# Windowed attention feeding a feed-forward block: wider input rows, block means on TensorE, a fused exponential, 120-column score products and a new instruction order

## The chip, the cores and the metric

The kernel runs on one core of one Trainium2 chip. A core has five engines with a queue each: TensorE (PE in the profile; its weight loads are PEld), VectorE (DVE), ScalarE (ACT), GpSimd (POOL) and SyncE (SP), which here issues every DMA. Each queue runs in order and waits for the others by semaphores. The metric is device time in microseconds (us), as a median of runs. All times in this part come from the kernel before the change: 655.01 us, median of 3 runs (654.32 to 655.39).

## What is computed

The reference has two parts, one behind the other. In numpy, cut to what matters:

```python
# q, k, v: (4, 8, 768, 64) fp32: batch, heads, tokens, head size
k_sum = k.reshape(B, H, 24, 32, 64).max(axis=3)      # 24 blocks of 32 tokens
v_sum = v.reshape(B, H, 24, 32, 64).mean(axis=3)
scores_l = scale * q @ k.T         # kept where |i - j| < 16, else -1e9
scores_s = scale * q @ k_sum.T + np.log(32)
a = softmax(concat([scores_l, scores_s]))            # the sum + 1e-9 divides
attn = a @ concat([v, v_sum])
x = attn.transpose(0, 2, 1, 3).reshape(3072, 512)
h = x @ w_in                       # (512, 2048)
out = (h * np.cos(h)) @ w_out      # (2048, 512)
```

So every query looks at its near tokens and at 24 summaries of the whole sequence; the result is the input of a feed-forward layer with a cosine gate.

## The kernel before

**Tiles.** The 3,072 tokens are cut into 8 blocks of 384; blocks 0 and 1 are the two halves of batch 0. The 8 heads are taken two at a time, so a block has four *groups*, which the order table calls `a`, `b`, `c`, `d`: `c0` is the third pair of heads in block 0. A group's 384 queries are cut into 6 tiles of 64. Each tile sees a window of 96 keys (64 and 16 on either side) and the 24 summaries, 120 columns in all.

**A group's steps**, with the names of the order table and the lines of the kernel before: load q, k, v (`q`, `k`, `v`, L436 to L479); turn q and k so that the head size lies on partitions (`tq`, `tk`, PE transposes with an identity, L493 and L506; from group `b2` on DVE does it in 32x32 squares); copy them out of PSUM (`cq`, `ck`), q times the scale; take the maxima of the k blocks (`ks`, L527); for blocks 0 and 1 put the mask into PSUM by a product with the identity (`ms`, L547); the scores (`sc`, L560); copy or scale them to SBUF (`z`); their maximum (`mx`, L579); subtract it on POOL (`su`, L584); the exponential on ACT (`ex`, L597); the row sums on DVE (`sm`, L600); their inverse (`iv`, L605); multiply by it on POOL (`nm`, L608); turn the probabilities (`tp` on PE and `cp`, or `pt`, `po`, `pi` by way of DRAM); the product with v (`va`, L661); and the split of the result into a high and a low part in a reduced fp32 format (`xh`, `xl`). The scores are two products for a tile and head, one with 96 keys and one with 24 summaries:

```python
for lo, n, key in ((0, W, k0), (W, NB, KW)):        # W = 96, NB = 24
    nc.tensor.matmul(out=self.sp[hh][s*QT:(s+1)*QT, c, lo:lo+n],
                     lhsT=self.qd[rows, t*QT:(t+1)*QT], rhs=self.kd[rows, key:key+n], ...)
```

The four combinations of head (64 partitions in) and tile parity (64 partitions out) use the four 64x64 quarters of TensorE. A value product uses all partitions in and 64 out, so two of them fit side by side.

**Summaries of v.** For batch 0, `v0_0` and `v0_1` load v once more with one block of 32 tokens in a partition (L248), POOL adds the two halves (L253) and DVE sums the rest (L263). Each group then fetches its 24 rows, repeated for 6 tiles, with two DMAs (`m`, L484). For batches 1 to 3 the loads come in quarters and POOL sums most of them.

**Weights.** w_in and w_out arrive as 64-bit floats. For each of 16 slices `w0` to `w15`, six steps on ACT, DVE and POOL (`ab`, `cl`, `sh`, `lb`, `fb` and then `hi`, `lo`) make two reduced fp32 parts out of 1 MB of raw bits.

**Feed-forward.** 128 steps `s0` to `s127`, one for a slice of 128 hidden columns and a block of tokens. `up` is 12 products with 384 columns (L705); then ACT, DVE, ACT, DVE form the gate (`tu` L715, `re` L718, `si` L723, `ga` L727), the result is split into `hi` and `lo`, and `dh`, `dl` are 9 products with 512 columns (L756). `s0` to `s5` and `s22` to `s31` are block 0, `s6` to `s21` block 1. The first `up` in the order is `s1`, and it needs all four groups of block 0 and the weight slice `w1`.

**Order.** The program records instructions by hand, in the order of one long table of tokens (`ORDER`); an engine runs its instructions in the order in which the table names them. `a0.tk.1.3` means: group a0, turn k, second half, PSUM bank 3; a last letter a, v or p says ACT, DVE or POOL.

Of the kernel before, what the change touches and what calls it, by code (L numbers as in the profile page):

```python
# [10 lines left out]
F32 = mybir.dt.float32  # L11
# [7 lines left out]
FUSED = "00000000000000000000000000000000"  # L19
# [14 lines left out]
w1.cl.v c0.iv a0.tp.1.0 d0.tq.1 w1.sh.2.3 d0.cq.a d0.ms.4.5 d0.sc a0.tp.0.1 w1.lb w1.fb.1 w0.ab.0 c0.nm c0.tp.0.2
w0.cl.v w1.hi.v w1.lo.p w0.sh.6.7 w0.lb a0.cp.1.a a0.cp.0.a d0.z.0.a b1.q a0.m w2.sh.0.1 w2.ab.0 d0.z.1.v d0.mx d0.su
a0.va.3 c0.tp.1.4 w0.fb.1 w0.hi.a w0.lo.p w2.cl.v w2.lb d0.ex d0.sm d0.iv b1.tq.5 d0.nm b0.ex c0.cp.0.a c0.cp.1.a
a0.xh.a w5.l w5.ab.0 a1.ms.6.7 w2.fb.1 b1.cq.v w2.hi.a w2.lo.p w5.cl.v a0.xl a1.q a1.tq.2 a1.cq.a w5.sh.0.1 b0.sm
c0.va.4 d0.m d0.tp.0.5 d0.cp.0.a d0.tp.1.2 d0.cp.1.a a1.sc w5.lb b0.iv b0.nm c0.xh.a w5.fb.1 c0.xl w3.l c1.q a1.z.0.a
# [138 lines left out]
def tile_kernel(  # L177
# [766 lines left out]
```

## Time and profile before

| | |
|---|---|
| median of 3 runs | 655.01 us |
| the profiled execution | 654.17 us |
| its span, first to last instruction | 652.4 us |
| mean granted TensorE clock | 0.990 |
| PE busy | 630.4 us, 97% of the span |
| DVE busy | 450.3 us, 69% |
| ACT busy | 304.1 us, 47% |
| POOL busy | 216.0 us, 33% |
| moved by DMA | 72.67 MB |

The profile is one execution. "x48" in a row counts instructions; a product of fp32 operands shows as two of them, a transpose as one. In a timeline row the first number is the start, the second the length; since products overlap in TensorE's pipeline, what a group costs is read from its start to the start of the next. In a group row the figures behind the bar are the busy time, the mean time of one in ns, and the idle time of the engine just before them.

### The profile page before, as it was taken

The page shows a single profiled execution, that of the slowest core. Times are in us where ns is not written, and L with a number is a line of the kernel's source. Part 1 is how long each engine was busy: PE and PEld are TensorE (multiplying, and loading weights), DVE is VectorE, ACT ScalarE, POOL GpSimd, SP SyncE. Part 2 cuts the span into 40 slices and gives each one's busy share as a digit, 9 for nine tenths or more (in the row PEclk, how much of TensorE's full clock was granted, in tenths as well). Part 3 has the DMA queues.
Part 4 walks back from the last instruction along what each step waited for, and adds up shares of the span by engine and source line. Part 5 has one row for each costly group of instructions (what it writes and reads, how often), then busy time and mean ns, then how long its engine had stood idle before and what let it go on. Part 6 is the DMA issues. An engine that isn't in the chain of part 4 may idle for free.

```text
span 652.4 us, 13154 instructions
## 1 busy us (share of the span) xinstructions
PE 630.4 (97%) x5141; PEld 558.6 (86%) x5141; DVE 450.3 (69%) x797; ACT 304.1 (47%) x503; POOL 216.0 (33%) x234
## 2 busy tenths in 40 slices
PE   5689999999999999999999999999999999999996
PEld 4458899988998899898898999798988998889895
DVE  4999989897677768667676567686676655543343
ACT  2598775656433534234564435434443453432332
POOL 4678854434332334213143334122230223301010
PEclk9789999999999999999999999999999999999999
DMA  9998633852244643451444442534343402410001
GB/s 218 278 269 248 205 105 110 235 131 43 67 125 115 182 98 103 93 101 56 110 112 118 121 124 79 108 60 105 96 124 83 112 25 63 111 40 33 0 1 48
DMA packets 167157, 72.67 MB, mean 111 GB/s; under 512 B 136824, under 2 KB 155832, under 8 KB 167096
## 3 DMA queue, kind: packets, MB, share of 16 engines
q1 hardware_dynamic: 167096, 71.84, 41.6%
q8 instruction: 40, 0.66, 0.4%
q14 instruction: 21, 0.17, 0.1%
HBM read 53.72 MB, written 15.73 MB: 106 GB/s over the span
## 4 chain that ended last, share of the span: by engine, by line
PE 88%; DVE 6%; ACT 1%; issue 1%; SPq 1%; POOL 1%; DMA 1%; ACTq 0%; DVEq 0%
PE banks L705 40%; PE banks L756 38%; PE banks L560 4%; PE banks L661 4%; PE banks L617 1%; SPq L447 1%; POOL w L350 1%; DVE kd L527 1%; DMA late<-in_k_dram 1%; PE banks L547 1%; DVE stage L406 1%; DVE vs L263 1%; DVE m L579 1%; DVE t L727 0%; DVE t L718 0%
## 5 line engine op out<-in xcount | busy, mean ns | idle before, releaser
L705 PE MATMUL banks<-xh,w 128*128 128x384 f32 x1024 | 268.6, 337 | 0.1
L756 PE MATMUL banks<-w,gh 128*128 128x512 f32 x768 | 198.0, 393 | 0.5 <-DVE gh L346 0.3
L705 PEld LDWEIGHTS banks<-xh,w 128*128 128x128 f32 x1024 | 185.5, 188 | 2.0 <-DVE sc L571 0.4
L705 PE MATMUL banks<-xl,w 128*128 128x384 f32 x512 | 171.3, 334 | 0.0
L756 PEld LDWEIGHTS banks<-w,gh 128*128 128x128 f32 x768 | 142.3, 188 | 31.3 <-DVE gh L346 2.0
L350 POOL TENSOR_TENSOR gl<-t,gh 128x384 fp32r<-128x384 f32 x55 | 57.3, 1043 | 223.9 <-DVE gh L346 107.6
L715 ACT ACTIVATE t<-banks 128x384 int32<-128x384 f32 x128 | 61.8, 489 | 143.9 <-PE banks L705 73.3
L718 DVE SCALAR_TENSOR_TENSOR t<-t,banks 128x384 f32<-128x384 int32 x128 | 69.4, 546 | 67.0 <-ACT t L715 66.3
L756 PE MATMUL banks<-w,gl 128*128 128x512 f32 x384 | 109.1, 392 | 0.1
L723 ACT ACTIVATE t<-t 128x384 f32<-128x384 f32 x128 | 66.2, 524 | 75.7 <-DVE t L718 75.1
L727 DVE TENSOR_TENSOR t<-t,banks 128x384 f32<-128x384 f32 x128 | 69.4, 548 | 43.4 <-ACT t L723 42.6
L705 PEld LDWEIGHTS banks<-xl,w 128*128 128x128 f32 x512 | 96.2, 188 | 0.4
L756 PEld LDWEIGHTS banks<-w,gl 128*128 128x128 f32 x384 | 71.5, 188 | 16.3 <-POOL gl L350 0.8
L608 POOL TENSOR_TENSOR sc<-sc,r 128x720 f32<-128x720 f32 x28 | 39.7, 1417 | 74.0 <-DVE r L605 73.1
L584 POOL TENSOR_TENSOR sc<-sc,m 128x720 f32<-128x720 f32 x28 | 39.2, 1403 | 72.4 <-DVE m L579 70.3
L350 DVE TENSOR_TENSOR gl<-t,gh 128x384 fp32r<-128x384 f32 x73 | 45.0, 620 | 16.7 <-ACT gh L344 10.4
L344 ACT CAST gh<-t 128x384 fp32r<-128x384 f32 x60 | 30.7, 511 | 39.5 <-DVE t L727 28.2
L346 DVE CAST gh<-t 128x384 fp32r<-128x384 f32 x68 | 28.3, 417 | 15.7 <-PE banks L756 12.4
L597 ACT ACTIVATE sc<-sc 128x720 f32<-128x720 f32 x28 | 22.5, 805 | 27.4 <-POOL sc L584 27.3
L560 PEld LDWEIGHTS banks<-kd,qd 64*64 64x64 f32 x1344 | 27.7, 132 | 8.1 <-issue 4.6
L253 POOL TENSOR_TENSOR kn<-kn 96x256 f32<-96x256 f32 (+1 forms) x36 | 23.3, 647 | 32.0 <-DMA kn<-in_v_dram 23.6
L560 PE MATMUL banks<-kd,qd 64*64 64x24 f32 (+1 forms) x1344 | 30.8, 231 | 1.3 <-DVE t L727 0.6
(99 smaller groups left out, 590.6 us busy)
## 6 DMA issues: line engine op xcount, KB each, us to landing
pd<-stage SPq DMA_DIRECT2D x22, 384.0 KB
late<-in_moe_w_in_dram SPq DMA_DIRECT2D x16, 512.0 KB
late<-in_moe_w_out_dram SPq DMA_DIRECT2D x16, 512.0 KB
pt<-pd SPq DMA_DIRECT2D x66, 96.0 KB
vn<-in_v_dram SPq DMA_DIRECT2D x52, 120.0 KB
out_dram<-stage SPq DMA_DIRECT2D x23, 256.0 KB
kn<-in_v_dram SPq DMA_DIRECT2D x24, 192.0 KB
qn<-in_q_dram SPq DMA_DIRECT2D x92, 48.0 KB
```

Source lines behind the costliest of these rows:

```text
L344: eng.copy(out=out, in_=in_)
L346: eng.tensor_copy(out=out, in_=in_)
L350: eng.tensor_tensor(out=lo, in0=src, in1=hi.bitcast(F32), op=ALU.subtract)
L560: nc.tensor.matmul(out=self.sp[hh][s * QT : (s + 1) * QT, c, lo : lo + n], lhsT=self.qd[rows, t * QT : (t + 1) * QT], rhs=self.kd[rows, ke ...
L584: nc.gpsimd.tensor_tensor(out=self.sc, in0=self.sc, in1=self.m.unsqueeze(2).broadcast_to([P, U, NK]), op=ALU.subtract)
L608: nc.gpsimd.tensor_tensor(out=self.sc, in0=self.sc, in1=self.r.unsqueeze(2).broadcast_to([P, U, NK]), op=ALU.mult)
L705: nc.tensor.matmul(out=self.h, lhsT=w_of(name, self.f)[:, c * P : (c + 1) * P], rhs=x_of(self.blk, part, c), start=n == 0, stop=n == last,)
L715: nc.scalar.activation(out=self.t.bitcast(I32), in_=self.h, func=AF.Copy, scale=1.0 / TWO_PI, bias=0.25)
L718: nc.vector.scalar_tensor_tensor(out=self.t, in0=self.t.bitcast(I32), scalar=-TWO_PI, in1=self.h, op0=ALU.mult, op1=ALU.add)
L723: nc.scalar.activation(out=self.t, in_=self.t, func=AF.Sin, scale=-1.0, bias=-0.5 * math.pi)
L727: nc.vector.tensor_tensor(out=self.t, in0=self.t, in1=self.h, op=ALU.mult)
L756: nc.tensor.matmul(out=self.acc[i], lhsT=g[:, i * P : (i + 1) * P], rhs=w_of(name, self.f), start=self.first and n == 0, stop=self.last an ...
```

## The change

1. Groups whose q and k are turned on PE load them in rows of 768 bytes: a partition takes three tokens that follow each other. A transpose of 128x128 then becomes two fp32 products with the identity, one for each head (`turn`), and the copies out of PSUM put the tokens back in order.
2. Batch 0's v means come from TensorE: `sum_v` (`vb`) multiplies the window tiles of v by a matrix `pairs` of 1/32, 6 products for a group of block 0 and 6 for the group of block 1 with the same heads, into one 24x128 tile in PSUM; `place_vs` (`vp`) copies it 6 times side by side into each group's v tile. The loads `v0_0`, `v0_1`, their sums and the `m` loads of blocks 0 and 1 are gone.
3. Blocks 0 and 1 hold the scores negated (q times -scale, the mask times -1); their exponential is 6 ACT instructions of 120 columns with the maximum as bias and the row sum as a second output. `su` and `sm` of these 8 groups are gone; `iv` has one small addition more.
4. In blocks 2 to 7 a copy of two instructions (`windows`, `kw`) lays windows and summaries of the 6 tiles side by side, and a score product has 120 columns. The copy lives where the second v tile was, so all groups of blocks 2 to 7 share one v tile and one window tile.
5. The order table is new, and `k_summaries` reads SBUF rather than PSUM.

```diff
-FUSED = "00000000000000000000000000000000"
+FUSED = "11111111000000000000000000000000"
 ORDER = """
-a0.k a0.tk.0.0 a0.ks.0 a0.ms.1.2 a0.tk.1.3 a0.q d0.k d0.tk.0.4 d0.ck.0.a a0.ck.0.a a0.tq.5 c0.k b0.k b0.tk.1.6
+a0.k a0.tk.1.7 a0.ck.1.a a0.tk.0.6 a0.ck.0.a a0.ms.5.4 a0.ks.1 a0.ks.0 d0.v c0.q a0.q c0.k c0.tk.1.3 a0.tq.1 a0.cq.a
...
+    minus = const.tile([P, P], F32, name="minus")
+    nc.scalar.mul(out=minus, in_=ident, mul=-1.0)
+    pairs = const.tile([P, 2 * NB - 1], F32, name="pairs")[:W]
+    nc.gpsimd.memset(pairs, 0.0)
+    nc.gpsimd.memset(pairs[:, NB - 2 : NB], 1.0 / BLOCK)
+    for j in range(2):
...
+        nc.gpsimd.affine_select(
...
-    vn0 = [const.tile([NK, U, P], F32, name=f"vn{i}") for i in range(2)]
+    vn0 = [const.tile([P, U, P], F32, name=f"vn{i}") for i in range(2)]
+    kw = vn0[1].rearrange("p u n -> p (u n)")[:, : U * NK].rearrange("p (u n) -> p u n", u=U)
...
-            for hh in range(2):
+            t = self.rows_of(t)
+            for half in range(t.shape[1]):
                 nc.sync.dma_start(
-                    out=t[:, :, hh * D : (hh + 1) * D],
-                    in_=src[2 * self.pr + hh].rearrange("(c p) d -> p c d", p=P),
+                    out=t[:, half].rearrange("p h c d -> p h (c d)"),
+                    in_=src[2 * self.pr : 2 * self.pr + 2, half * TB : (half + 1) * TB].rearrange(
+                        "h (p c) d -> p h (c d)", p=P
+                    ),
                 )
...
+        def sum_v(self, *i):
+            if i:
+                self.vb = groups[1][self.pr].vb = bank(*i)[W:NK, :P]
+            for t in range(U):
+                j = 2 * (U * self.half + t)
+                nc.tensor.matmul(
+                    out=self.vb, lhsT=pairs[:, NB - 2 - j : 2 * NB - 2 - j], rhs=self.vn[:W, t, :],
+                    start=j == 0, stop=j == NB - 2,
+                )
+        def place_vs(self, eng):
+            copy(eng, self.vn[W:NK], self.vb.unsqueeze(1).broadcast_to([NB, U, P]))
...
+        def turn(self, to, rows):
             for c in range(QC):
-                nc.tensor.transpose(out=self.qT[:, c * P : (c + 1) * P], in_=self.qn[:, c, :], identity=ident)
+                for h in range(2):
+                    nc.tensor.matmul(
+                        out=to[h * D : (h + 1) * D, c * P : (c + 1) * P], lhsT=rows[:, h, c], rhs=ident,
+                        start=True, stop=True,
+                    )
...
+        def windows(self, eng):
+            self.kw = kw
+            wide = bass.AP(self.kd.tensor, self.kd[:, self.base :].offset, [self.kd.ap[0], [QT, U], [1, W]])
+            copy(eng, kw[:, :, :W], wide)
+            copy(eng, kw[:, :, W:], self.kd[:, KW:].unsqueeze(1).broadcast_to([P, U, NB]))
...
+            if self.kw is not None:
+                for t in range(U):
+                    c, s = divmod(t, 2)
+                    for hh in range(2):
+                        rows = slice(hh * D, (hh + 1) * D)
+                        nc.tensor.matmul(
+                            out=self.sp[hh][s * QT : (s + 1) * QT, c, :],
+                            lhsT=self.qd[rows, t * QT : (t + 1) * QT], rhs=self.kw[rows, t, :],
+                            start=True, stop=True,
+                        )
+                return
...
-        groups.append([Group(blk, i, vn0[i % 2], sc0[:, i % 2]) for i in range(NG)])
+        groups.append([Group(blk, i, vn0[0], sc0[:, i % 2]) for i in range(NG)])
```

The exponential of a fused group is not new code; `FUSED` only selects it:

```python
for u in range(U):
    nc.scalar.activation(out=self.sc[:, u, :], in_=self.sc[:, u, :], func=AF.Exp,
                         bias=self.m[:, u : u + 1], scale=-1.0, accum_out=self.r[:, u : u + 1])
```

What the new table moves is shown at three places. The first is SP's queue at the start of the program. Before it stand the loads of k and q of all groups first (`late`, `kn` and `x` are the tiles that hold them), and then v for the sums; brackets name what a row waits for, DMAHW being an earlier DMA:

```order
L447 DMA late_127<-in_k_dram 128x6x64 x2
L447 DMA late_128<-in_q_dram 128x3x64 x2
L447 DMA kn<-in_k_dram 128x6x64 x2
L447 DMA x_2_137<-in_k_dram 128x6x64 x2
L447 DMA late_127<-in_k_dram 128x6x64 [waits DMAHW0_49]
L447 DMA late_127<-in_k_dram 128x6x64 [waits DMAHW1_49]
L248 DMA late_126<-in_v_dram 96x1024 [waits DMAHW2_49]
```

At the same place in the changed program, `x_1` is the v tile of group d0, whose edge rows POOL clears in the set-up:

```order
L466 DMA late_136<-in_k_dram 128x2x192 x2
L495 DMA x_1_145<-in_v_dram 96x5x64 x2
L503 DMA x_1_145<-in_v_dram 80x2x64 [waits Pool_49]
L466 DMA late_139<-in_q_dram 128x2x192
L466 DMA late_137<-in_q_dram 128x2x192
L466 DMA x_2_146<-in_k_dram 128x2x192
```

The v load of d0 now stands behind the first k, and the third of its DMAs, which waits for POOL, stands ahead of every q and of the other k loads. The second place is PE's queue behind the scores of d0, the last of block 0, up to the first scores of block 1. Before (`pt` and `vn` or `x` are probabilities and v; `ident,sc` and `ident,late` are transposes):

```order
L617 MATMUL banks<-ident,sc 120x128 x4
L617 MATMUL banks<-ident,late_130 120x128 x4
L661 MATMUL banks<-pt,vn_103 64x64 x12
L617 MATMUL banks<-ident,late_130 120x128 x2
L493 MATMUL banks<-ident,late_129 128x128 x3
L547 MATMUL banks<-mask,ident 128x360 x2
L493 MATMUL banks<-ident,late_128 128x128 x3
L661 MATMUL banks<-pt,x_0_135 64x64 x12
L617 MATMUL banks<-ident,late_130 120x128 x6
L560 MATMUL banks<-kd_99,qd 64x96
```

After, `pairs` is the matrix of the block sums and `minus` the negative identity:

```order
L523 MATMUL banks<-vn_112,pairs 24x128 x6
L523 MATMUL banks<-late_137,pairs 24x128 x6
L673 MATMUL banks<-ident,sc 120x128 x6
L673 MATMUL banks<-ident,late_139 120x128 x2
L538 MATMUL banks<-ident,late_137 64x128 x6
L717 MATMUL banks<-pt,vn_112 64x64 x12
L592 MATMUL banks<-mask,minus 128x360 x2
L523 MATMUL banks<-x_0_144,pairs 24x128 x6
L538 MATMUL banks<-ident,late_139 64x128 x6
L616 MATMUL banks<-kd_108,qd 64x96
```

The block sums of v stand ahead of the first values and between the turns, and only one value product is left ahead of block 1's first scores. The third place is ACT's queue in the same stretch. Before, from ACT's copy of d0's scores on (`stage` and `banks` rows of 1024 columns are steps of the weight slices):

```order
L344 COPY late_130<-banks 128x3x120
L394 ACTIVATE banks<-late_125 128x1024
L382 ACTIVATE stage_411<-late_125 128x1024
L344 CAST w_433<-stage_431 128x1024
L597 ACTIVATE late_130<-late_130 128x6x120
L597 ACTIVATE sc<-sc 128x6x120
L344 COPY pt<-banks 120x512
L344 COPY pt<-banks 120x256
L344 CAST xh_0_451<-banks 128x384
```

After, from the copy of the block means of a0 on (24x768):

```order
L362 COPY vn_112<-banks 24x768
L400 ACTIVATE stage_453<-late_140 128x1024
L362 COPY pt<-banks 120x256
L412 ACTIVATE banks<-late_140 128x1024
L362 COPY late_137<-banks 24x768
L362 CAST xh_0_484<-banks 128x384
L362 COPY pt<-banks 120x256
L548 ACTIVATE qd<-banks 128x384
L400 ACTIVATE stage_494<-late_134 128x1024
L648 ACTIVATE late_139,r<-late_139,m 128x120 x6
```

Copies of block means have come in, and an exponential is a row of six.

More of the change, by code (lines that the diff above doesn't have):

```diff
@@ L34 @@
[L34 to L38, printed above, removed]
@@ L258, in v_summaries @@
         if first:
-            vsum[b, hg] = att.tile([P, D], F32, name=f"vs{hg}")[: HG * NB]
+            vsum[b, hg] = att.tile([P, D], F32, name=f"vs{hg}", bufs=2)[: HG * NB]
         out_t = vsum[b, hg]
         if eng is nc.vector:
-            to = out_t if first else kmax.rearrange("p n t -> p (n t)")[: t.shape[0], :D]
+            to = out_t if first else part_sum[: t.shape[0]]
             eng.tensor_reduce(out=to, in_=t.rearrange("p (j d) -> p d j", d=D), axis=AX.X, op=ALU.add)
@@ L278, in tile_kernel @@
     make_identity(nc, ident)
+    minus = const.tile([P, P], F32, name="minus")
[4 more added lines that the diff above has]
+    for j in range(2):
+        rows, first = pairs[:, NB - 2 + j : NB - 1 + j], WINDOW + j * BLOCK
+        nc.gpsimd.affine_select(
+            out=rows, in_=rows, pattern=[[0, 1]], compare_op=ALU.is_ge, fill=0.0, base=-first, channel_multiplier=1,
+        )
+        nc.gpsimd.affine_select(
+            out=rows, in_=rows, pattern=[[0, 1]], compare_op=ALU.is_ge, fill=0.0, base=first + BLOCK - 1,
+            channel_multiplier=-1,
+        )
     mask = const.tile([P, QC + 1, NK], F32, name="mask")
@@ L301, in tile_kernel @@
     qd0 = const.tile([P, TB], F32, name="qd")
-    kmax = const.tile([P, NB // 2, BLOCK // 2], F32, name="kmax")
+    part_sum = const.tile([P, D], F32, name="part_sum")
     kd = [const.tile([P, KW + NB], F32, name=f"kd{i}") for i in range(NPAIR)]
-    vn0 = [const.tile([NK, U, P], F32, name=f"vn{i}") for i in range(2)]
+    vn0 = [const.tile([P, U, P], F32, name=f"vn{i}") for i in range(2)]
+    kw = vn0[1].rearrange("p u n -> p (u n)")[:, : U * NK].rearrange("p (u n) -> p u n", u=U)
+    vn0 = [t[:NK] for t in vn0]
     NKP = -(-(NK + 1) // SQ) * SQ
@@ L547, in place_masks @@
                 nc.tensor.matmul(
-                    out=sp, lhsT=ident, rhs=mask[:, self.half : self.half + QC, :], start=True, stop=False
+                    out=sp, lhsT=minus if self.fused else ident, rhs=mask[:, self.half : self.half + QC, :], start=True, stop=False
                 )
```

327 lines of the change are left out of this document (165 added, 162 removed).

## The prediction

> **What bounds the kernel now.** I read the page's busy times first, then windows cut where the work changes: at the end of the scores of d0, at the first `up`, at the `up` of s5, and at the tail. Columns of a window row: length, then busy time (and instructions) of PE, PEld, DVE, ACT, POOL, the granted clock, the DMA share and GB/s.
>
> ```profile
> PE 630.4 (97%) x5141; PEld 558.6 (86%) x5141; DVE 450.3 (69%) x797; ACT 304.1 (47%) x503; POOL 216.0 (33%) x234
> ...
> 0.00:30.21 30.21, 18.84 (x246) 14.01 (x246) 20.90 (x34) 9.65 (x16) 16.14 (x41) 0.89 0.97 243
> 30.21:54.35 24.14, 19.75 (x345) 14.34 (x339) 23.35 (x31) 22.02 (x36) 17.27 (x10) 0.93 0.90 263
> 54.35:79.14 24.79, 24.79 (x217) 22.15 (x213) 23.87 (x43) 20.77 (x32) 20.61 (x14) 1.00 0.83 247
> 79.14:630.00 550.86, 549.57 (x4268) 493.63 (x4265) 374.45 (x677) 245.13 (x408) 159.04 (x169) 1.00 0.36 95
> 630.00:652.40 22.40, 17.40 (x82) 14.44 (x80) 7.76 (x15) 6.49 (x13) 2.90 (x3) 0.95 0.10 35
> ```
>
> From 54 us to 630 us PE is never idle for more than 1.3 us in all: there time is the sum of PE's work. Ahead of 54 us PE idles, and DVE is the full engine (23.35 of 24.14 us), with DMA beside it (0.90 to 0.97). So the change is worth two things: how much later or earlier the dense stretch begins, and how much PE work lies in it. The cuts are these PE rows:
>
> ```profile
> 4.46 0.87 PE L506 MATMUL banks<-ident,late 128*128 128x128 f32 x3 [4.46 <-DMA late<-in_k_dram]
> ...
> 29.20 1.09 PE L560 MATMUL banks<-kd,late 64*64 64x96 f32 x48
> ...
> 54.35 0.45 PE L705 MATMUL banks<-xh,w 128*128 128x384 f32 x1
> ...
> 79.14 0.44 PE L705 MATMUL banks<-xh,w 128*128 128x384 f32 x1
> ```
>
> The third window of the timeline gives the price of every PE step of a group, from start to start:
>
> ```profile
> 43.69 0.55 PE L493 MATMUL banks<-ident,late 128*128 128x128 f32 x3
> 44.07 1.38 PE L547 MATMUL banks<-mask,ident 128*128 128x360 f32 x4
> 45.38 0.92 PE L661 MATMUL banks<-pt,x 120*64 120x64 f32 x24
> 46.25 0.63 PE L617 MATMUL banks<-ident,sc 128*120 128x128 f32 x4
> 46.81 1.09 PE L560 MATMUL banks<-kd,qd 64*64 64x96 f32 x48
> 47.83 0.43 PE L617 MATMUL banks<-ident,sc 128*120 128x128 f32 x2
> 48.10 1.38 PE L547 MATMUL banks<-mask,ident 128*128 128x360 f32 x4
> ```
>
> A turn costs 0.38 (0.127 a pass of 128 columns), masks 1.31, values 0.87, scores 1.02, the transposes of the probabilities 0.56 + 0.27.
>
> **PE ahead of the first up.** Before: 16 turns x 0.38 = 6.1, 8 masks x 1.31 = 10.5, 8 scores x 1.02 = 8.2, 4 sets of transposes x 0.83 = 3.3, 4 of values x 0.87 = 3.5: 31.6 us. PE starts at 4.5, so 18.3 of the 54.35 us are waiting and a slow clock (0.89, 0.93).
>
> A turn becomes 6 fp32 products, 12 passes of 128 columns, by heads on two column halves. Bounds: 6 x 0.127 = 0.76 if the halves run side by side, 12 x 0.127 = 1.52 if not. The nearest row is the values: 24 passes of 64 columns, also two halves, take 0.87, 36 ns each where half of 127 is 64, so they do overlap. I take 0.8: 16 x 0.42 = +6.7. The block sums of v are 8 x 12 passes of 128 columns, all on the same columns of the array, nothing beside them: 12 x 0.127 = 1.5, 8 of them +12.2 (at least half of that, were they to overlap). All stand ahead of the first `up`. PE's work there becomes 31.6 + 6.7 + 12.2 = 50.5; from 4.5 on that ends at 55.0 with no wait at all. So of the 18 us of idle PE time the change spends nearly all before anything is gained.
>
> **DVE and POOL** are relieved.
>
> ```profile
> L600 DVE TENSOR_REDUCE r<-sc 128x6 f32<-128x726 f32 x28 | 25.1, 898 | 7.0 <-ACT sc L597 6.9
> L263 DVE TENSOR_REDUCE vs<-late 96x64 f32<-96x1024 f32 x2 | 3.8, 1896 | 0.0
> L584 POOL TENSOR_TENSOR sc<-sc,m 128x720 f32<-128x720 f32 x28 | 39.2, 1403 | 72.4 <-DVE m L579 70.3
> L253 POOL TENSOR_TENSOR late<-late 96x1024 f32<-96x1024 f32 x2 | 4.7, 2352 | 8.2 <-DMA late<-in_v_dram 8.2
> ```
>
> DVE loses 8 sums x 0.9 and 3.8 for v, 11 us, and gains two copies of block means and 8 small additions, some 3; POOL loses 8 x 1.4 + 4.7 = 15.9. DVE, which set the start, no longer does. The loads of 1.5 MB of v and 16 small DMAs go too. What is late next is ACT.
>
> **ACT.**
>
> ```profile
> L597 ACT ACTIVATE sc<-sc 128x720 f32<-128x720 f32 x28 | 22.5, 805 | 27.4 <-POOL sc L584 27.3
> L597 ACT ACT_TABLE_LOAD x19 | 24.4, 1283 | 0.3
> L382 ACT ACTIVATE stage<-late 128x1024 f32<-128x1024 f32 x16 | 18.6, 1161 | 3.5 <-DVE banks L398 3.2
> L394 ACT ACTIVATE banks<-late 128x1024 int32<-128x1024 uint8 x16 | 17.9, 1116 | 0.1
> L344 ACT CAST w<-stage 128x1024 fp32r<-128x1024 f32 x12 | 12.5, 1044 | 4.0 <-DVE stage L406 3.9
> L344 ACT CAST xh<-banks 128x384 fp32r<-128x384 f32 x15 | 7.3, 485 | 5.1 <-PE banks L661 5.1
> L344 ACT COPY pt<-banks 120x256 f32<-120x256 f32 x10 | 3.8, 376 | 2.6 <-PE banks L617 2.6
> L344 ACT COPY pt<-banks 120x512 f32<-120x512 f32 x6 | 3.5, 588 | 0.0
> L344 ACT COPY sc<-banks 128x360 f32<-128x360 f32 x6 | 2.8, 485 | 6.9 <-PE banks L560 6.9
> L499 ACT ACTIVATE qd<-banks 128x384 f32<-128x384 f32 x3 | 1.5, 497 | 0.9 <-PE banks L493 0.9
> ```
>
> No row shows the fused exponential. From 805 ns for 720 columns and 485 for 360, a column is 0.89 ns and the fixed part 165, so 120 columns take 0.27, six 1.6; six of the 256-column row would be 2.26, an upper bound if bias and sum are free. I take 2.0, against 0.8 now. The Trainium skill, *ScalarE: Activation LUTs*, under *What ACT_TABLE_LOAD costs*, gives an ACTIVATE with a pointer bias about 280 ns and 0.833 ns a column, an estimate of 2.3 for the six, which would put the first `up` 0.6 later; no run here shows it yet.
>
> A copy of block means has 768 columns: 0.85 by the 720-column row. From the first of them to the last `xh` ahead of the first `up`, ACT's queue holds 5 x 1.16 + 5 x 1.12 + 1.04 (weights), 2 exponentials 4.0, 4 more mean copies 3.4, 7 copies of probabilities 4 x 0.38 + 3 x 0.59 = 3.3, 6 score copies 2.9, 4 q copies 2.0, 3 `xh` 1.5: 29.5, and 0.85 for the first copy itself. It cannot begin before PE has done d0's scores and 12 block-sum products behind them (3.0). Behind that copy in ACT's queue wait the weights of w0 and all of block 1's copies. PE's work up to d0's scores is 12 turns x 0.8 + 4 x 1.31 + 4 x 1.02 = 18.9, so 23.4 at the earliest; before it was 13.9 and ended at 30.2. What lies between is loads:
>
> ```profile
> 1.82 1.07 SPq L447 DMA_DIRECT2D late<-in_q_dram  x2
> ...
> 4.92 0.34 POOL L847 MEMSET x<- 120x128 f32 x2
> ...
> masks.py:199 POOL TENSOR_SCALAR_AFFINE_SELECT ident<-ident 128x128 f32<-128x128 f32 x1 | 0.3, 293 | 0.1
> ```
>
> SP's second load used to go out at 1.82. Now d0's edge rows of v wait there for POOL's set-up, which cleared the `x` tiles by 5.26 and has six more small instructions ahead of them (0.1 to 0.3 each): 5.9 to 7. Every q and the other three k queue behind. I put the end of d0's scores at 26.5, about halfway. Then 26.5 + 3.0 + 0.85 + 29.5 = 59.9, and 0.5 of DVE for `xl`: first `up` at 60.4 where it was 54.35, **+6.0** (bounds +0.5, PE's own sum, and +10, d0's scores no earlier than before).
>
> **From there to s5**, 24.8 us before, PE's work stays the same to within 1 us. ACT had 20.8; four exponentials add 4 x 1.2, the last mean copy 0.85, so 26.4, with table loads between Exp and Sin as many as now or one more (1.28). PE's waits for it: **+1.5** (0 to +5).
>
> **The dense stretch.** The steady rows are the same as at the start:
>
> ```profile
> 204.76 0.92 PE L661 MATMUL banks<-pt,vn 120*64 120x64 f32 x24
> 205.61 1.09 PE L560 MATMUL banks<-kd,qd 64*64 64x96 f32 x48
> 206.63 0.44 PE L705 MATMUL banks<-xh,w 128*128 128x384 f32 x1
> ```
>
> 48 passes of scores take 1.02. With 24 passes of 120 columns each quarter streams the same 6 x 120 columns, 0.71 at 0.127 for 128; so at least 0.7 and at most 1.02. The values, 12 passes a half, lose 0.85 - 12 x 0.064 = 0.08 beyond their streams. I take 0.8: 24 groups x 0.22 = -5.3. Group a2's two k turns add 0.8. Together **-4.5** (-6.9 to +0.8). The 24 window copies (720 columns, about 1 us on ACT or DVE) hide: DVE has 176 us free in the 551 and ACT 306. Without that cover they would be 24 us. The tail's last matmul to the end is built as before: 0.
>
> **Sum:** +6.0 + 1.5 - 4.5 = +3.0 on the profiled execution (654.17, span 652.4): 657.2. The median of the runs shown is 655.01, 0.84 above it; so 658.0.
>
> **Rivals.** Less than 0.2% (1.3 us) is what a measurement here can tell from no change; the three runs lie 1.1 apart.
>
> *The start packs tightly* (faster): PE instead of ACT sets the first `up`, at 55.0, because the six exponentials take 1.6 and the late loads are absorbed by the v sums and masks. Then +0.6 + 0 - 4.5 = -3.9: 651.1. It decides once d0's scores end before 22. For it: DMA, 0.97 busy ahead of 30 us, loses the extra v, and DVE has room. Against: PE would have to run its 50.5 us without a gap while each group comes back to it from ACT. Chance 0.27.
>
> *The terms cancel* (no change): first `up` at 58, waits to s5 under 1: 655. Chance 0.13.
>
> *My forecast*: 0.45, with its own range 656.3 to 663.
>
> *One v tile and one window tile* (slower): a group's v can be loaded only when the values before it are done, and it queues on SP behind stores.
>
> ```profile
> PE banks L661 <- DMA vn<-vs: 2.1, 1, 2.1
> ```
>
> That wait came once, at the start. If every fifth of 23 changes of group paid it, 5 x 2.1 = +10: 668. Against it: between two value sets the new order keeps at least 8.9 us of products on PE, by the prices above. Chance 0.08.
>
> *Column halves do not overlap* (slower): turns at 1.52, 0.72 dearer. Then 16 of them raise PE's own sum from 55.0 to 66.5, 6.1 behind my first `up`, and a2's three add 2.2: 666. The values' 36 ns a pass speak against it. Chance 0.07. The Trainium skill, *TensorE: Matmul & The Clock Gate*, *Part 3: Packing small matmuls — row/col tiling*, says that a weight load overlaps running products only where the row group differs; the two heads' halves share all rows, so by that rule the turns, and the values too, would serialize. The trace of the values disagrees.
>
> *The wider rows do nothing seen*: PE waits for k's landing only at the start, and the queue decides that; this is inside the forecast.
>
> Slower 0.45 + 0.08 + 0.07 = 0.60. The range leaves out the best scores with a packed start (below 651) and half of the last two rivals: 651 to 666.
>
> **What would show it.** Right: the first `up` near 60, ACT at 95% or more between d0's scores and that, DVE below it, q and k issued only after 5 us; score sets of 24 passes (line 604 of the changed kernel) lasting about 0.8. Wrong: a first `up` ahead of 56, exponentials under 0.27 each, or block sums under 1 us; or, the other way, the values (line 717) waiting for v loads again and again.

## The result and the profile after

The changed kernel takes 666.67 us (median of 4 runs, 664.11 to 667.0) against 655.2 for the kernel before on the same chip (4 runs, 654.32 to 656.41): a ratio of 1.0165, 95% interval 1.0135 to 1.0196. It is slower by 11.5 us; the forecast was 3.0 slower, and 666.67 lies 0.7 above the range's end. The profiled execution took 666.37, its span is 664.6, so 12.2 more than before. One execution further down, the profiled one of the half-and-half kernel in experiment 11, took 785.85 us at a granted clock of 0.75; no time is read from it.

The page's busy times of the changed kernel, and then its windows, cut at the same events as before (end of d0's scores, first `up`, s5's `up`, tail):

```profile
PE 644.7 (97%) x4832; PEld 565.2 (85%) x4832; DVE 435.4 (66%) x781; ACT 341.9 (51%) x643; POOL 231.5 (35%) x255
```

```profile
0.00:30.05 30.05, 22.90 (x352) 18.09 (x352) 11.99 (x25) 13.20 (x40) 7.06 (x41) 0.94 0.91 228
30.05:65.20 35.15, 32.58 (x474) 24.82 (x472) 30.49 (x37) 29.20 (x64) 14.88 (x8) 0.95 0.85 217
65.20:94.93 29.73, 26.63 (x231) 22.66 (x226) 24.78 (x44) 26.75 (x76) 18.45 (x19) 1.00 0.35 118
94.93:642.00 547.07, 544.86 (x3703) 484.34 (x3700) 359.05 (x660) 265.72 (x451) 187.06 (x185) 1.00 0.37 95
642.00:664.60 22.60, 17.77 (x86) 15.28 (x84) 9.12 (x18) 7.00 (x14) 4.01 (x4) 0.94 0.10 36
```

| stretch | before | after | difference | forecast |
|---|---|---|---|---|
| start to the end of d0's scores | 30.21 | 30.05 | -0.2 | -3.7 |
| from there to the first `up` | 24.14 | 35.15 | +11.0 | +9.8 |
| first `up` to s5's | 24.79 | 29.73 | +4.9 | +1.5 |
| s5's `up` to the end | 573.26 | 569.67 | -3.6 | -4.5 |
| sum | 652.4 | 664.6 | +12.2 | +3.0 |

The dense stretch came out nearly as forecast. The start did not. There no engine stands out: between d0's scores and the first `up` PE is busy 93% of the time, DVE 87%, ACT 83%, where ACT had been forecast at 95%. Counted from start to start of its rows, PE spent 11.3 us of this stretch on the block sums and 1.1 more than before on turns, while its waits fell from 4.4 to 2.6. The prices of PE's new steps, from start to start:

```profile
19.83 0.88 PE L538 MATMUL banks<-ident,kn 128*64 128x128 f32 x12
20.53 0.82 PE L538 MATMUL banks<-ident,late 128*64 128x128 f32 x12
...
30.05 1.49 PE L523 MATMUL banks<-vn,pairs 96*24 96x128 f32 x12
31.38 1.47 PE L523 MATMUL banks<-late,pairs 96*24 96x128 f32 x12
32.78 0.87 PE L673 MATMUL banks<-ident,sc 128*120 128x128 f32 x6
...
174.74 0.85 PE L604 MATMUL banks<-vn,qd 64*64 64x120 f32 x24
175.51 0.92 PE L717 MATMUL banks<-pt,vn 120*64 120x64 f32 x24
```

A turn is 0.70 (forecast 0.8), a set of block sums 1.33 to 1.40 (1.5), a score set 0.77 (0.8). A pass of a turn so takes 0.058, half of the 0.117 that a pass of the block sums takes at 1.40: the two column halves of a turn do overlap. The Trainium skill, *TensorE: Matmul & The Clock Gate*, *Part 3: Packing small matmuls — row/col tiling*, says that a weight load overlaps running products only where the row group differs; the two halves share all rows, and this trace does not agree. One of the six-part exponentials on ACT, with its last row's end:

```profile
45.62 0.40 ACT L648 ACTIVATE sc<-sc,m 128x120 f32<-128x120 f32 x1
45.91 0.19 ACT L648 ACTIVATION_READ_ACCUMULATOR sc<-sc,m 128x1 f32 x1
46.01 0.39 ACT L648 ACTIVATE sc<-sc,m 128x120 f32<-128x120 f32 x1
...
47.80 0.19 ACT L648 ACTIVATION_READ_ACCUMULATOR sc<-sc,m 128x1 f32 x1
47.90 1.13 ACT L412 ACTIVATE banks<-late 128x1024 int32<-128x1024 uint8 x1
```

It takes 2.28 us (forecast 2.0): each part is followed by an instruction that reads out the row sum, which no row of before could show. So the single prices were near. What went wrong lies between the engines.

### The profile page after: what moved, and what is told of

It reads as the page before. It is cut to its first block, busy times and chain, and to the rows that moved or that the text cites. A ratio compares the mean times of both kernels' runs of the same rounds, so it can differ in the third digit from the quotient of the medians.

```text
span 664.6 us, 12660 instructions
## 1 busy us (share of the span) xinstructions
PE 644.7 (97%) x4832; PEld 565.2 (85%) x4832; DVE 435.4 (66%) x781; ACT 341.9 (51%) x643; POOL 231.5 (35%) x255
## 4 chain that ended last, share of the span: by engine, by line
PE 81%; DVE 6%; ACT 4%; DMA 2%; issue 1%; SPq 0%; POOL 0%; DVEq 0%; ACTq 0%
PE banks L812 37%; PE banks L761 36%; PE banks L717 3%; PE banks L604 3%; DMA late<-in_moe_w_in_dram 1%; ACT late L648 1%; ACT sc L648 1%; DVE stage L424 1%; DVE m L635 1%; DMA kn<-in_k_dram 1%; PE banks L538 0%; DVE stage L405 0%; DVE t L774 0%; ACT stage L400 0%; ACT t L779 0%
## 5 line engine op out<-in xcount | busy, mean ns | idle before, releaser
L368 POOL TENSOR_TENSOR gl<-t,gh 128x384 fp32r<-128x384 f32 x69 | 71.2, 1036 | 205.8 <-ACT gh L362 81.2
L812 PEld LDWEIGHTS banks<-w,gl 128*128 128x128 f32 x384 | 71.6, 188 | 15.8 <-DVE gl L368 0.8
L362 ACT CAST gh<-t 128x384 fp32r<-128x384 f32 x71 | 36.1, 511 | 47.3 <-DVE t L783 24.4
L640 POOL TENSOR_TENSOR sc<-sc,m 128x720 f32<-128x720 f32 x24 | 33.6, 1401 | 58.1 <-DVE m L635 58.1
L368 DVE TENSOR_TENSOR gl<-t,gh 128x384 fp32r<-128x384 f32 x59 | 36.5, 619 | 23.1 <-PE banks L812 14.8
L368 POOL TENSOR_TENSOR w<-stage,w 128x1024 fp32r<-128x1024 f32 x13 | 31.9, 2455 | 29.8 <-ACT w L362 15.3
L627 DVE SCALAR_TENSOR_TENSOR sc<-banks,mask 128x360 f32<-128x360 f32 x48 | 24.4, 523 | 15.9 <-PE banks L604 15.4
L254 POOL TENSOR_TENSOR kn<-kn 96x256 f32<-96x256 f32 (+1 forms) x38 | 25.0, 659 | 22.6 <-DMA kn<-in_v_dram 21.1
L364 DVE CAST gh<-t 128x384 fp32r<-128x384 f32 x57 | 22.4, 393 | 12.0 <-PE banks L812 9.9
```

The source lines that it names most:

```text
L254: eng.tensor_tensor(out=t[:, :n], in0=t[:, :n], in1=t[:, n:], op=ALU.add)
L362: eng.copy(out=out, in_=in_)
L368: eng.tensor_tensor(out=lo, in0=src, in1=hi.bitcast(F32), op=ALU.subtract)
L627: eng.scalar_tensor_tensor(out=out, in0=self.sp[hh], scalar=-SCALE if self.fused else SCALE, in1=mask[:, self.half : self.half + QC, :], o ...
L640: nc.gpsimd.tensor_tensor(out=self.sc, in0=self.sc, in1=self.m.unsqueeze(2).broadcast_to([P, U, NK]), op=ALU.subtract)
L812: nc.tensor.matmul(out=self.acc[i], lhsT=g[:, i * P : (i + 1) * P], rhs=w_of(name, self.f), start=self.first and n == 0, stop=self.last an ...
```

## The experiments

All times are medians beside runs of the kernel before on the same chip (654.5 to 655.3); ratios are to that kernel, with their 95% interval. "First `up`" and "s5's `up`" are read from each profiled execution.

| kernel | us | ratio | first `up` | s5's `up` |
|---|---|---|---|---|
| changed kernel | 666.67 | 1.0165 | 65.20 | 94.93 |
| d0's v loaded later | 660.85 | 1.0088 (1.0067 to 1.0108) | 59.59 | 89.34 |
| old turns | 663.03 | 1.0124 (1.0104 to 1.0145) | 63.20 | 92.59 |
| both of these | 658.86 | 1.0053 (1.0036 to 1.0070) | 58.84 | 88.22 |
| both, fewer block sums | 656.76 | 1.0036 (1.0022 to 1.0051) | 59.06 | 88.50 |
| both, one exponential | 657.17 | 1.0027 (1.0001 to 1.0052) | 58.26 | 83.69 |
| both, both taken away | 652.46 | 0.9966 (0.9949 to 0.9984) | 56.42 | 81.86 |

**1. d0's v loaded later.** One token of the order table moves; the v load of d0 no longer stands ahead of the loads of q and k:

```diff
-a0.ks.0 d0.v c0.q a0.q c0.k ...
+a0.ks.0 c0.q a0.q c0.k ... d0.q d0.v
```

> The changed kernel with the v loads of d0 issued behind d0's q instead of ahead of every q and the other three k. If SP's wait for POOL's set-up (until 6.1 us) holds the start, q and k are issued 2 to 3 us earlier, TensorE's wait of 2.60 us at 9.7 goes, and the time falls by 2 to 3 us: 664. If the transfers themselves or the work behind them set the pace, the wait moves elsewhere and the time stays within 0.7 us.

SP's queue in the changed kernel, first, and then in this one:

```profile
1.81 1.00 SPq L495 DMA_DIRECT2D x<-in_v_dram  x2
6.14 0.31 SPq L503 DMA_DIRECT2D x<-in_v_dram  x1
6.50 0.96 SPq L466 DMA_DIRECT2D late<-in_q_dram  x2
```

```profile
1.81 0.98 SPq L465 DMA_DIRECT2D late<-in_q_dram  x2
2.83 0.98 SPq L465 DMA_DIRECT2D x<-in_k_dram  x2
```

and its first `up`:

```profile
59.59 0.45 PE L760 MATMUL banks<-xh,w 128*128 128x384 f32 x1
```

SP stood still from 2.81 to 6.14 for POOL's set-up. Without that, d0's scores end at 24.5 in place of 30.05, the first `up` comes 5.6 earlier and the time falls by 5.8: twice what was expected, and more than the 3.3 us of the hold. PE's rows show where the rest lies, in the changed kernel and then in this one:

```profile
12.31 0.88 PE L538 MATMUL banks<-ident,x 128*64 128x128 f32 x12 [2.60 <-DMA x<-in_k_dram]
13.02 3.53 PE L538 MATMUL banks<-ident,late 128*64 128x128 f32 x36
```

```profile
8.99 0.88 PE L537 MATMUL banks<-ident,x 128*64 128x128 f32 x12
9.69 2.13 PE L537 MATMUL banks<-ident,late 128*64 128x128 f32 x36
```

Ahead of the end of d0's scores PE idled 7.15 us in the changed kernel (30.05 less 22.90 of work) and 4.04 here (24.45 less 20.41). So 3.1 of the 5.6 are waits, and 2.5 are the same instructions taking longer: the three turns behind the wait show 3.53 against 2.13, and the clock granted between 14.3 and 16.3 us was 0.50, where this kernel shows 1.00 throughout. The hold of one queue is the largest single cause found, half of what the change costs.

**2. Old turns.** The loads of q and k in 256-byte rows and the transposes are back (`load_heads`, `turn`, `place_q`, `place_k` as before):

```diff
-                for h in range(2):
-                    nc.tensor.matmul(out=to[h*D:(h+1)*D, c*P:(c+1)*P], lhsT=rows[:, h, c], rhs=ident, ...)
+                nc.tensor.transpose(out=to[:, c * P : (c + 1) * P], in_=rows[:, c, :], identity=ident)
```

> The changed kernel with the loads of q and k in rows of 256 bytes and 128x128 transposes again; the rest and the order stay. If TensorE sets the start, 16 turns x (0.70 - 0.38) = 5 us go ahead of the first up, which comes near 60, and the time falls by 4 to 5 us: 662. If ACT sets it, first up and time stay within 1 us. If the rows of 768 bytes had made the loads faster, q and k land later again and the gain is eaten: d0's scores would end at 30 or later still.

The time falls by 3.6, the first `up` by 2.0. That is the 2.0 by which d0's scores end earlier (28.1); the four turns behind them, 1.3 us of TensorE, brought nothing to the first `up`. Another 1.1 lies behind s5's `up`, where the three turns of a2 became cheaper.

**3. Both** (1 and 2 in one kernel):

> The changed kernel with d0's v loads behind d0's q and with the rows of 256 bytes and the 128x128 transposes. If the two are separate terms, 660.9 - 3.6 = 657.3. If without SP's hold TensorE's turns lie in front of nothing (its wait goes up as its work goes down), 660.5 or more. If the short rows land late, d0's scores end behind 24.5.

658.86: the turns are worth 2.0 once the hold is gone. In the trace d0's scores end 2.5 earlier than in kernel 1 (21.9), but the first `up` only 0.75 earlier. In between two loads come late that kept nobody waiting so long in kernel 1:

```profile
21.83 1.11 ACT L399 ACTIVATE stage<-late 128x1024 f32<-128x1024 f32 x1 [4.17 <-DMA late<-in_moe_w_out_dram]
24.29 1.51 PE L519 MATMUL banks<-vn,pairs 96*24 96x128 f32 x12 [2.37 <-DMA vn<-in_v_dram]
```

This kernel is the base of the next three.

**4. Fewer block sums**, 2 of each 6 products:

```diff
-            for t in range(U):
+            for t in range(0, U, U - 1):
```

> The kernel with d0's v loads later and 128x128 transposes (658.9), with 2 of the 6 products of each set of block sums: two thirds of the sum of v are left out, all copies and waits stay. TensorE loses 8 x 8 passes, 7.5 to 8.4 us. If TensorE's own sum sets the start, the first up comes from 58.8 to 51 to 53 and the time to 651 to 653. If ACT's queue sets it, as the prediction had it, the first up stays within 2 us: 657 to 659.

TensorE's block sums went from 12.6 to 4.9 us. The median fell by 2.1, with intervals that overlap the base's, and in the profiled execution the first `up` stayed. That execution took 660.43, 3.7 above the median, so it shows where the freed time can go, not where it usually goes. The stretch ahead of it in the base and in this kernel:

```profile
21.91:58.84 36.93, 31.41 (x437) 23.82 (x436) 31.00 (x39) 33.81 (x79) 15.26 (x8) 0.95 1.04 268
```

```profile
21.89:59.06 37.17, 27.22 (x372) 19.14 (x372) 32.89 (x39) 33.97 (x79) 14.75 (x8) 0.86 1.02 252
```

Its TensorE rows that wait for ACT:

```profile
27.00 1.47 PE L665 MATMUL banks<-ident,sc 128*120 128x128 f32 x6 [1.62 <-ACT sc L361]
...
39.48 1.60 PE L584 MATMUL banks<-mask,minus 128*128 128x360 f32 x4 [3.07 <-ACT sc L361]
```

Of the 7.7 us taken away, TensorE's busy time lost only 4.2, and that turned into waits, mostly for ACT; the other 3.5 went into a lower clock, 0.86 where the base had 0.95. In this execution TensorE's sum does not set the start, though in the base it was 85% busy; ACT is at 91 to 92% in both.

**5. One exponential** in place of six:

```diff
-                for u in range(U):
-                    nc.scalar.activation(out=self.sc[:, u, :], ..., bias=self.m[:, u : u + 1], scale=-1.0, accum_out=...)
+                nc.scalar.activation(out=self.sc, in_=self.sc, func=AF.Exp, scale=-1.0)
```

> The kernel with d0's v loads later and 128x128 transposes (658.9), with one plain exponential of 720 columns where the fused one has six: the subtraction of the maximum and the row sum are left out, nothing takes their place on POOL or DVE (the small addition reads the maxima instead). ACT loses 8 x 1.55 us. If ACT's queue sets the start and the waits behind the first up, the time falls by 5 to 9 us, to 650 to 654. If TensorE sets the start, only the wait ahead of block 1's masks (2.1) and the two behind the first up (2.7) can go: 655 to 658.

The subtraction of the maximum and the row sum are left out. The runs spread (651.87 us at a mean granted clock of 1.000 to 659.34 at 0.985), while the median falls by 1.7, again with overlapping intervals; the profiled execution took 654.59, 4.2 less than the base's, and is read for where that lies. Ahead of the first `up`, 0.6. Behind it, the five steps to s5's `up` take 25.4 in place of 29.4, close to the 24.8 of the kernel before:

```profile
58.26:83.69 25.43, 25.25 (x220) 22.46 (x216) 24.92 (x44) 20.74 (x32) 16.46 (x18) 1.00 0.43 135
```

PE is full there. So the four exponentials of block 1 are what makes the first steps wait; the next kernel shows the same 25.4. The start itself is not set by ACT's exponentials alone either.

**6. Both taken away** (4 and 5):

> The kernel with d0's v loads later and 128x128 transposes, with both taken away: 4 of 6 products of each set of block sums (their part of the v means is left out) and the six-part exponential (maximum and row sum are left out). TensorE loses 7.7 us, ACT 12.4. Each alone left the first up where it was (59.1, 58.3). If each was hidden behind the other, the first up now comes at 50 to 54. If DVE (33 of 36 us busy with the one exponential) holds it, 56 to 58, and the time is that of the one exponential, 656 to 658, less 1.

```profile
21.38:56.42 35.04, 27.36 (x372) 18.63 (x372) 32.21 (x39) 29.62 (x46) 15.26 (x8) 0.85 1.08 256
```

The first `up` comes at 56.4, in the band that was given for DVE, and DVE is at 92%. The time, 652.46, is 6.4 below the base and 4.3 to 4.7 below each alone, more than that band had; each alone gave 2.1 at most. Here the profiled execution (652.25) stands for the median: 2.4 of the 6.4 lie ahead of the first `up` and 4.0 in the five steps behind it. That both give more than the sum of each fits TensorE, ACT and DVE standing so near each other that taking work from one hands the wait to the next. It is not shown beyond that: the traces of 4 and 5 lie 3.7 above and 2.6 below their medians. One rival is untested: in kernels 3 to 6 the DMA engines are full ahead of the first `up` (shares of 1.02 to 1.08), and the two late loads of kernel 3 are there in 4 to 6 as well (3.2 to 4.5 us on ACT, 1.3 to 2.8 on PE). No run here takes loads away.

**7. The exponential undone** in the changed kernel: `FUSED` to zeros, `su` behind each `mx`, `sm` behind each `ex` for the 8 groups.

> The changed kernel with the fused exponential of blocks 0 and 1 undone: POOL subtracts the maximum, one ACT exponential of 720 columns per group, DVE sums the rows; all else stays. ACT loses 8 x 1.5 us. If ACT sets the start (the theory on record), the first up comes from 65.2 to 60 or earlier and the time falls by 7 to 9 us, to about 658. If TensorE's own added work sets it, the first up can only lose the one long wait of TensorE there (2.08 us at 44.57) and the slow clock behind it (1.6): not before 61.5, and the time falls by 2 to 6 us, most of it from waits behind the first up: 661 to 665.

674.16 (1.0291, 1.0268 to 1.0314), 7.5 slower, against both expectations. The first `up` comes at 70.27:

```profile
38.61 0.68 PE L673 MATMUL banks<-ident,late 128*120 128x128 f32 x2 [6.09 <-POOL late L664]
```

With the subtraction back on POOL, POOL's multiplication is late. In this order the fused form relieves POOL and DVE by more than it costs ACT; the table was not laid for a subtraction on POOL.

**8. The v loads back** in the changed kernel: `v0_0`, `v0_1` and their sums, `m` where `vb` stood, `vp` gone.

> The changed kernel with batch 0's v means as before the change: loaded block by block, summed by POOL and DVE, fetched by the m loads; no block sums on TensorE, no copies of means. If TensorE sets the start, its 8 x 1.37 us go and the first up comes at 55 to 59, the time falls by 6 to 10 us: 657 to 661. If ACT sets it, only its copies of means go (7 x 0.8, of which 3.4 ahead of the first up): about -3 to -4, 663. If the v loads and sums were the limit of the kernel before, DVE and POOL take the start back and nothing is gained: 665 to 668.

673.14 (1.0272, 1.0246 to 1.0297), 6.5 slower. TensorE waits 8.53 us ahead of the first values (48.75). The row names no releaser, but those values read the tile that the `m` loads fill, and these go out only at 41.75, behind loads of weights and v on SP, though the sums were done at 31.6. And d0's scores end 4 later. The row of that wait:

```profile
48.75 0.58 PE L716 MATMUL banks<-pt,vn 120*64 120x64 f32 x4 [8.53 <-issue]
```

The new table was not laid for these loads, so this tells nothing on the price of the block sums themselves.

**9. Two score products again**: the `kw` tokens dropped.

> The changed kernel without the window copies: two products (96 and 24 columns) for a tile and head in blocks 2 to 7 again. TensorE's share of the scores of these blocks is 24 x 0.78 us with 120 columns against 24 x 1.02 before; if the dense stretch is the sum of TensorE's work, the time rises by 24 x 0.24 = 5.8 us, to 672.5. If the window copies (24 us on ACT and DVE) or the single v tile had been paid for by waits, less: 667 to 670.

671.74 (1.0243, 1.0216 to 1.0270), 5.1 slower than the changed kernel. TensorE's time for all scores, summed from start to start over the trace, goes from 27.8 to 33.4, 24 x 0.23. The gain of the dense stretch is real.

**10. b1's copy of means earlier** (on kernel 1):

```diff
-... a1.nm w4.lo.v s1.up.3 d1.z.0.a s1.tu b1.vp.a ...
+... b0.va.2 b0.xh.a b1.vp.a b0.xl ...
```

> The changed kernel with d0's v loads behind d0's q, and with ACT's last copy of block means (b1) ahead of two fused exponentials instead of behind them. It is the copy that frees the bank in which s2's up starts. If that copy behind the exponentials is what TensorE waits for behind the first up (2.7 us in two waits), they go and the time falls by 2 to 2.7: 658.5. If the wait passes on to the next work on ACT, within 0.7 of 660.9.

662.73, 1.9 slower than kernel 1. Of the two waits for ACT the longer (1.6) went, but 1.7 for POOL and 1.1 for DVE came in its place.

**11. Can the gain be had without the start?** Eight kernels bear on it; none beats the kernel before.

*120 columns alone* on the kernel before (window copies; one v tile, so 25 loads of v and means move behind the values of the group before):

> The kernel before with the 120-column products alone (window copies on ACT and DVE by turns; one v tile for blocks 2 to 7, so 25 v and m loads move behind the values of the group before). Start as before the change. If the gain of the dense stretch is separate from the new start: 655.1 - 5.8 = 649.3. If the single v tile makes the values wait (five times 2.1 us, the rival of the prediction), 655 to 660.

678.67 (1.0359, 1.0329 to 1.0390). The scores gain 5.0, but TensorE waits 22 us more, 10.6 of them for probabilities that come late by way of DRAM. That they are late because SP's queue now stands at the v loads ahead of them is read from the order of the queue, not tested. From TensorE's waits (us in total, times, longest):

```profile
PE banks L681 <- DMA pt<-pd: 10.6, 2, 6.3
```

*Half and half*: the table before up to s7, the new one from there with the 120-column products and the one v tile, and no other part of the change.

```diff
-... s5.st.2 v1_3.l w11.l s11.up.6 s9.up.7 s8.up.4 ...
+... s5.st.2 a2.tq.6 a2.cq.v v1_3.l v1_3.s.v ... s8.up.6 s8.tu ...
```

> Half and half: instructions and order of the kernel before up to step s7, then the order of the changed kernel for everything else, with the 120-column products and one v tile. No block sums on TensorE, no fused exponential, 128x128 transposes. If the start alone costs the 11.5 us and the rest of the change saves what its stretch shows (10th up to the end: 554.9 us against 560.0 before), the first up stays at 54.4 and the time is 655.2 - 5 = 650 (649 to 651). If the new order of the rest only works behind the new start, 655 or more.

660.21 (1.0079, 1.0063 to 1.0094). Three parts of the change were put on it, one at a time: rows of 768 bytes with the new turns, the fused exponential (`FUSED`, the negated scores, `su` and `sm` dropped), and the v means by TensorE (`vb`, `vp` ahead of the values).

> The half-and-half kernel with q and k in rows of 768 bytes and two fp32 products for a transpose as its only other edit (and the maxima of k behind the copies). TensorE gains 16 x 0.32 + 3 x 0.35 = 6 us; the 15.8 us that it waits ahead of the first up can take 5 of them. If those waits absorb the turns, within 1.5 us of the half-and-half kernel; if TensorE's sum decides, 4 to 6 slower; if the wider rows land earlier, faster.

> The half-and-half kernel with the fused exponential in blocks 0 and 1 as its only other edit. DVE was full ahead of the first up (23.35 of 24.14 us) and loses 8 x 0.9, POOL 8 x 1.4; ACT (22.02 of 24.14) gains 8 x 1.55. If DVE and POOL hold the start, 2 to 5 us faster than the half-and-half kernel; if ACT becomes the bound, as the prediction had it, 3 to 7 us slower.

> The half-and-half kernel with batch 0's v means by TensorE as its only other edit: no v0 loads, no sums on POOL and DVE, no m loads for blocks 0 and 1; 8 sets of 12 passes (11.3 us of TensorE) and 8 copies (6.3 us of ACT), v of block 1 loaded early. If TensorE's sum decides the start, 5 to 11 us slower than the half-and-half kernel; if the relief of DVE, POOL and DMA pays for it, within 2 us or faster.

661.83, 669.19 and 676.64 (672.32 to 680.73). Alone in the old order, the new turns cost 1.6, of the 6 us of work that was expected, the fused exponential 9.0, the block sums 16. With 7 this says that the exponential's sign depends on the order around it: it helps in a table laid for it, and costs in the other.

At the seam an `up` waits for the copy of a2's q (7.2 us at 101.1 in the kernel with the wider rows), so that turn was moved behind s9's down products:

> The half-and-half kernel with one step moved at its seam: the turn of a2's q (and its copy by DVE) behind s9's down products and into another bank, since s8's up waited 7.2 us for that copy, which stood behind DVE's weight steps. If that wait is all that kept the half-and-half kernel above 650, 660.2 - 7.2 = 653 or a little less, faster than the kernel before. If DVE's backlog there holds TensorE in any case, 657 or more.

660.35: that wait went, and three others came (1.4, 4.7 and 2.1 us at 93, 100 and 127), two for DVE's steps of weight slices and the longest for a copy on ACT that had itself stood behind DVE. A seam at s31, with all weights made:

> The kernel before, word for word, up to the values of d2 (step s31), and from there the order of the changed kernel with 120-column products and one v tile for 19 of the 24 later groups; no other part of the change. TensorE spends 19 x 0.245 = 4.7 us less on scores. If that gain is separate from the start and all weights are made by then, so that no work is late at the seam, 654.5 - 4.7 = 650 (649 to 651.5), faster than the kernel before. If the new order needs its own start, 655 or more.

673.25 (1.0292, 1.0268 to 1.0316), by one wait, for the addition of s31, which DVE has behind sums of v whose loads the two tables place differently:

```profile
230.99 0.69 PE L725 MATMUL banks<-xh,w 128*128 128x384 f32 x1 [18.08 <-DVE stage L793]
```

With these loads spread:

> The late half-and-half kernel with its seam mended: s34's up waited 18.1 us there for DVE's addition behind a chain of five loads and sums of v (batch 2), which the old order does later and the new one earlier than the seam. These loads now stand among steps s26 to s31, the addition and the next ups ahead of the waiting work. If the seam's waits were all, 650 to 652; if the seam keeps 3 us or more, 653 to 656; each way the stretch from the 61st up to the end should last 313 to 316 us against 319.4 before.

657.43 (1.0041, 1.0025 to 1.0056): waits of 0.8 to 2.9 us at the seam remain. Behind the seam the gain is always there: in every kernel with the new order and 120 columns whose times are read, the 61st `up` to the end (counting 12 products of 384 columns to an `up`) takes 314.5 to 315.2 us, against 319.4 before.

## Why the prediction was wrong in size

The direction held, and so did two of the mechanisms: slower, by a start in which SP holds the loads, less a gain in the scores. That ACT alone would then fill the start did not hold. The sum of 9.2 us that was missing lies in these steps.

- **"I put the end of d0's scores at 26.5, about halfway."** This step failed, by 3.5: 30.05. SP's hold was seen, and its bounds (5.9 to 7 for its end) held: 6.14. But its price was guessed as a middle between 23.4 and 30.2. Experiment 1 measures it: 5.6 us at d0's scores and the same at the first `up`. The next q went out at 6.50, 4.7 us behind its place in experiment 1, and the rest queued behind it. The sum also took every step of PE at its price at the full clock: 2.5 of the 5.6 are not waiting but rows made longer by the lower clock behind the wait.
- **From d0's scores to the first `up`**: forecast 33.9, measured 35.15. Near, but not by the chain given. ACT was 83% busy, not 95%, and PE, which the forecast gave room, was 93% busy: before, 11.4 of PE's 15.8 idle us lay ahead of the end of d0's scores and only 4.4 behind it, where all block sums stand. "DVE, which set the start, no longer does" is not borne out either: ahead of the first `up` DVE was to lose 11 and gain 3, and went from 44.25 (20.90 + 23.35) to 42.48 (11.99 + 30.49). Of the eight row sums only four had stood ahead of the first `up`:

```profile
L600 DVE TENSOR_REDUCE r<-late 128x6 f32<-128x726 f32 x2 | 1.8, 899 | 0.0
L600 DVE TENSOR_REDUCE r<-sc 128x6 f32<-128x726 f32 x2 | 1.8, 893 | 0.0
```

With 5.9 for v the loss was 9.5; two copies of means (1.9), two more weight copies (1.4), the additions of `iv` (1.9) and holds by POOL (3.0, last section) took 8.2 of it back. In the traces of experiments 4 to 6 neither PE's sum nor the exponentials alone set it. How the 5.2 us that the start is still late without SP's hold (59.59 against 54.35) divide is not settled: the turns are 0.75 of them, the exponentials with two thirds of the block sums 2.4, and the cause of the other 2.1 stays open.
- **"PE's waits for it: +1.5 (0 to +5)."** Measured +4.9, at the end of its bounds. Here the mechanism was right and the size off: ACT had 26.75 us of work (forecast 26.4) in what was then 24.8 + 1.5 = 26.3, which left its queue no gap at all. It had 3.0 of gaps, the longest (1.0) for PE's values; and PE's longest wait, 1.6, is for ACT's last copy of block means. Experiment 5 gives back 4.0. PE's waits are 3.1 of the 4.9; a2's q turn, 0.7, moved in, and the rest, 1.1, is PE work at slightly longer starts.
- **The dense stretch**: -4.5 forecast, -3.6 measured, of which the scores -5.3 (as forecast), the two k turns of a2 and its transposes +1.0, waits +0.8.

The rivals: the packed start, at 0.27, needed d0's scores before 22. That came true only in experiments 3 to 6 (21.4 to 21.9), and even there the first `up` was at 56 to 59, so PE would not have set it. That one v tile makes the values wait (0.08) did not happen in the new order; where the old order is kept (11), TensorE waits 22 us more, 10.6 of it for probabilities. That column halves do not overlap (0.07) is refuted by the turns, at 0.70. Of the signs listed, "q and k issued only after 5 us" and "score sets about 0.8" came true; "first `up` near 60" and "ACT at 95% or more" did not.

## What to carry to other kernels

An instruction that waits on an in-order DMA queue costs what everything behind it loses, not the length of its wait: 3.3 us of standing cost 5.8 here, in part through the clock behind TensorE's wait, and one moved token gave them back. Where three engines are each 83 to 93% busy, take work from one in an experiment before you name it the bound; the freed time may only become a wait for the next. And an effect of 2 us isn't read from one execution that lies 3.7 from its median. A part of a change is worth what it is worth in the order it was laid for: the same exponential was 7.5 us good in one table and 9.0 bad in the other.

## What the runs showed of the hardware

A simple DVE operation can be held by POOL. DVE's clamp of 1024 columns takes 0.68 us; beside a POOL addition it shows 2.85, and a DVE addition of 6 columns (0.16 alone) shows 1.39. DVE and POOL in the changed kernel:

```profile
34.91 2.85 DVE L405 TENSOR_SCALAR stage<-stage 128x1024 f32<-128x1024 f32 x1
...
41.66 0.69 DVE L405 TENSOR_SCALAR stage<-stage 128x1024 f32<-128x1024 f32 x1
43.21 1.39 DVE L660 TENSOR_SCALAR r<-r 128x6 f32<-128x6 f32 x1 [0.87 <-ACT late L648]
...
50.24 0.89 DVE L635 TENSOR_REDUCE m<-sc 128x6 f32<-128x720 f32 x1
```

```profile
34.84 2.36 POOL L368 TENSOR_TENSOR w<-stage,w 128x1024 fp32r<-128x1024 f32 x1 [2.25 <-DVE w L364]
...
41.82 2.75 POOL L368 TENSOR_TENSOR w<-stage,w 128x1024 fp32r<-128x1024 f32 x1 [4.62 <-DVE w L364]
...
49.20 2.37 POOL L368 TENSOR_TENSOR w<-stage,w 128x1024 fp32r<-128x1024 f32 x1 [2.84 <-DVE r L660]
```

The two long ones end 0.6 us and at once after POOL does (37.20 and 44.57). It goes both ways: POOL's addition at 41.82, begun while a clamp ran, takes 2.75, and the one at 49.20 only 2.37. And not every DVE operation is held: the maximum of 720 columns at 50.24 takes 0.89 beside POOL's addition, and 0.89 at 37.68 with POOL idle. The groups of the clamp ahead of the first `up`, before and after:

```profile
L387 DVE TENSOR_SCALAR stage<-stage 128x1024 f32<-128x1024 f32 x6 | 4.4, 732 | 0.0
```

```profile
L405 DVE TENSOR_SCALAR stage<-stage 128x1024 f32<-128x1024 f32 x6 | 7.4, 1226 | 1.4 <-ACT stage L400 1.2
```

So 3.0 us of DVE's relief went there. The Trainium skill, *SBUF — State Buffer*, under *SBUF: two separate sides*, calls the ports that the two engines share an exclusive lock, held for a whole instruction. The rows above agree with that.

The read-out of the accumulator is an instruction of its own, 0.19 us; with it the six parts of an exponential repeat every 0.38.

TensorE's granted clock was halved for some microseconds behind most of its longer waits. In windows of 2 us from the end of the wait, the changed kernel shows 0.81, 0.50 and 0.83 behind the wait of 2.60 at 12.31, and the kernel of experiment 4 shows 0.81, 0.50, 0.50 and 0.50 behind its wait of 3.07 at 39.48. Behind the wait of 1.62 at 71.26 of the changed kernel the clock stays at 1.00; but so it does behind one of 2.57 at 42.15 in kernel 6, and what decides between these is not shown. The busy share alone does not: ahead of the end of d0's scores kernel 1 was 83% busy at 1.00, and in its next stretch 93% busy at 0.95.
